# A small GpSimd write ahead of the first gather, and half of the second round of proposals later in VectorE's queue

## The chip, the cores and the metric

The kernel is one program on one core of a Trainium2 chip. The metric is the device time of the whole launch in microseconds (us). One core has five queues that concern us: TensorE (PE, with its weight loads PEld), VectorE (DVE), ScalarE (ACT), GpSimd (POOL) and SyncE (SP), and DMA queues which SP, ACT and POOL feed. [...]

## The reference, cut to what matters

```
scores = cap * tanh(q @ k.T / sqrt(64) / cap)      # 8 x 12 heads, 448 x 448
x = softmax(scores) @ v  -> (3584 tokens, 768)
logits = x @ w_gate                                 # 3584 x 8 experts
order = argsort(-logits.flatten())
for tok, e in order:                                # greedy: the largest logit first
    if assigned[tok] < 0 and counts[e] < 448: assigned[tok] = e; counts[e] += 1
for e in range(8):                                  # two products for the expert's 448 tokens
    out[mask_e] = relu(x[mask_e] @ w1[e]) @ w2[e]
```

## The kernel before

**Three stages.** Attention fills the first 350 us or so and writes x into a DRAM buffer `xs`. The routing finds, round by round, which expert is full first and which 448 tokens it gets. Each round starts with proposals: every token still free proposes itself to its best expert, as keys of three parts (`VA`, `VB`, `VC`, and the sums `K1`, `K2`); a search over the keys then finds the threshold. The FFN of the expert found in round p runs on TensorE while VectorE and ScalarE search round p+1 between the products.

**Proposals.** `propose_a` (12 VectorE instructions on all 3584 tokens, laid out 112 x 32) makes `m`, `P`, `kk`, `At`, `VA` and the raw parts `b` and `c`. `propose_b` (6 instructions, lines 514 to 518 and 526) makes `Bt`, `Ct`, `VB`, `VC`, `K1` and `K2` out of them. `propose` calls both, one behind the other. Which comes first needed: `VA` is turned by TensorE (line 536) and copied by VectorE (`VAt`, line 541) for the first search steps ("A"). `VB` and `VC` are turned by TensorE behind search step A0 (`flips`, into `psV`); `K1` and `K2` are used steps later.

**The seam between routing and FFN.** Round 0 ends with `idx` (line 722), the row numbers of expert 0's 448 tokens, from VectorE. GpSimd then issues the first gather: four indirect DMAs (line 872) of 128, 128, 128 and 64 rows of `xs` into the tiles `xg`. A dummy indirect DMA (`frow`, line 793) stands ahead of them. TensorE in the meantime runs 23 warming products (`warm(NW)`), turns `VA`, and then transposes the gathered rows, 128 at a time (`tx`, line 879). The first two of the four go through `cutx` (ScalarE makes the rounded part `xgh`, VectorE the rest `xgl`, lines 928 and 929), and `first` (line 895) multiplies them with expert 0's first weights; then come the other two, and `ffn1(0, 0)` (line 966), in which two more transposes (`xtr`, line 902) stand. The search steps of round 1 stand in TensorE's queue between the products of `ffn1`; each is one small product (line 572) that waits for VectorE's and ScalarE's comparisons (`cmpD`, lines 564 and 566, and `cmpA`, line 560), and its result is read by `fl` (line 576).

**What sets the order.** The order in each queue is the order of the Python calls: SP, PE, ACT, DVE and POOL are all under a manual schedule here. Waits come from data and from memory: a tile that takes the memory of an earlier one waits for that one's last readers and writers. `xg` takes memory that attention's tiles had, so the first gather waits not only for `idx` and the five DMA counters of the writes into `xs`, but also for a TensorE product of attention (line 236).

Of the kernel before, what the change touches and what calls it, by code (L numbers as in the profile page):

```python
# [6 lines left out]
F32=mybir.dt.float32; F32R=mybir.dt.float32r; BF16=mybir.dt.bfloat16; F16=mybir.dt.float16; I32=mybir.dt.int32; I16=mybir.dt.int16  # L7
# [378 lines left out]
class Routing:  # L386
# [357 lines left out]
    def phases0(s,wp,L,turned):  # L744
        HA=[7,10]; HB=3
        for p in range(s.E):
            s.hA=HA[min(p,len(HA))-1] if p else 7; s.hB=HB; s.na=2 if p<9 else 1
            s.cur=p
            if p:
                s.propose(L,0,s.NC)  # L750
                yield 30
            yield from (s.search(wp,turned if p==0 else ()) if p<s.E-1 else s.last(wp))
            yield -((p-1)*320+LK[p]) if p>1 else 4
            yield from s.finalise(wp,L,p<s.E-1)
# [3 lines left out]
def ffn_all(nc, tc, ctx, rt, xs, xz, wg, w1, w2, out, ident, E, wp, deferred, xctx, gen, avs):  # L758
# [16 lines left out]
    def need(p):  # L775
        while len(res)<=p: step()
# [51 lines left out]
    fp=ctx.enter_context(tc.tile_pool(name="fp",bufs=1))  # L828
# [33 lines left out]
    def newx(p):  # L862
        if p not in xgT: xgT[p]=(fp.tile([128,DC,C],F32R,name="xgh"),fp.tile([128,DC,C],F32R,name="xgl"))
    xgp=[fp.tile([128,2*DM],F32,name=f"xg{k}") for k in range(2)]
    row=lambda j,n=128: xgp[j//2][:n,j%2*DM:(j%2+1)*DM]
    nc.scalar.activation(xgp[1][64:128,DM:],rt.zero[64:128].broadcast_to([64,DM]),AF.Copy)
    def gather(p):
        if p>=E or p in xgs: return
        need(p)
        xgs[p]=1  # L870
        for j,(o,n) in enumerate(TS):
            g=nc.gpsimd.indirect_dma_start(out=row(j,n),out_offset=None,in_=xs,in_offset=bass.IndirectOffsetOnAxis(ap=res[p][0][:n,j:j+1],axis=0))
        return g
# [22 lines left out]
    def xtr(p,c):  # L896
        if p>=E or c is None: return
        newx(p)
        gather(p)
        ps=pt.tile([128,512],F32,name="psX")  # L900
        for j,(o,n) in enumerate(TS):
            nc.tensor.transpose(ps[:,o:o+128],row(j)[:,c*128:c*128+128],ident)
        cutx(p,c,ps)
# [21 lines left out]
    def cutx(p,c,ps,c0=0,c1=C):  # L925
        h,l=(t[:,c,c0:c1] for t in xgT[p])
        src=ps[:,c0:c1]
        nc.scalar.activation(h,src,AF.Copy)
        nc.vector.tensor_tensor(l,src,h.bitcast(F32),op=ALU.subtract)  # L929
# [5 lines left out]
    def tick(n=1):  # L935
        cnt[0]+=n; bc[0]+=n; now[0]+=n
        if bc[0]>=BG:
            if pend and not (cur[0]==FT-1 and 144<now[0]%320<316): bc[0]=0; scatter(*pend.pop(0))
        if len(res)>cur[0]+1 and cur[0]+1 not in xgs:
            bc[0]=0; n=cur[0]+1; gather(n)  # L940
            if n>=FT:
                xq.extend((now[0]+TD+TJ*j,lambda j=j: planes(j)) for j in range(4))
                xq.extend(((n-1)*320+248+8*f,lambda f=f: split1(n,f)) for f in range(2))
                o=(n-1)*320; g=now[0]-o; a=max(262,g+92); b=max(284,g+118)
                bg.extend((o+x,o+min(y,316),z) for x,y,z in ((a,a+18,lambda: cutt(n,0,0,3)),(a,a+34,lambda: cutt(n,0,3,6)),(b,b+(0 if n==FT else 26),lambda: cutt(n,1,0,3)),(b,b+(7 if n==FT else 22),lambda: cutt(n,1,3,6))))
        while xq and xq[0][0]<=now[0]: xq.pop(0)[1]()
        if bg and bg[0][1]<=now[0]: bg.pop(0)[2]()
        if cnt[0]>=hint[0]:
            cnt[0]=0; step()
    hh={}  # L950
    def ffn1(p,f,work):
        if f==0: hh[p]=f2.tile([128,FC,2*C],F32R,name="hh")
        wh,wl=spl.pop((p,1,f))
        xh,xl=xgT[p]
        ps=acc.pop(0) if p==0 and f==0 else ph.tile([128,512],F32,name="psH")
        m=0
        seq=[(c,k) for c in range(DC) for k in range(3)]
        if p==0 and f==0:
            seq=[(0,0),(0,2)]
            for c in range(1,DC): seq+=[(c,0),(c,2),(c-1,1)]  # L960
            seq+=[(DC-1,1)]
        elif p>=FT and f==0: seq=[(c,k) for c in range(DC) for k in (0,2)]+[(c,1) for c in range(DC)]
        for c,k in seq:
            a,b=((wh,xh),(wh,xl),(wl,xh))[k]
            o=256 if p==0 and f==0 and c<4 else 0
            nc.tensor.matmul(ps[:,o:C],a[:,c,:],b[:,c,o:],start=(m==0 and o==0),stop=(m==DC*3-1)); m+=1  # L966
            if p==0 and f==0 and k==1 and c<2: xtr(0,c+4)
            tick()
            for z in work.get(m,()): z()
        end[0]=now[0]  # L970
        h=hh[p][:,f,:]
        nc.scalar.activation(h[:,:C],ps[:,:C],AF.Relu)  # L972
        for a,b,d in ((384,448,448),(0,384,512)):
            nc.vector.scalar_tensor_tensor(h[:,d:d+b-a],ps[:,a:b],0.0,h[:,a:b].bitcast(F32),op0=ALU.max,op1=ALU.subtract)  # L974
# [35 lines left out]
    need(0)  # L1010
    WG=3; NW=23; WJ=4
    gather(0)
    tok=xgp[1][0:1,0:1]
    for i in range(WG,W1B): load1(0,i,tok)
# [8 lines left out]
    for p in range(E):  # L1023
        lastp=p==E-1; cur[0]=p
        for f in range(FC):
            if p==0:
                if f<2: load1(0,f+W1B)
                if f<7: load2(0,f+1)
                if 2<=f<4: load1(0,f+W1B)
            else:  # L1030
                if f<6: load2(p,f+2)
                if W1B<=f+W1B-1<FC: load1(p,f+W1B-1)
            work={}
            if f+2<FC and (p,1,f+2) not in spl: work[3]=[lambda: split1(p,f+2)]
            at={0:{1:[(11,0)],2:[(11,1)],3:[(11,2)],4:[(11,3)],5:[(11,4)],6:[(3,5),(11,6)],7:[(3,7)]},1:{k:[(11,k)] for k in range(FC)},2:{**{k:[(11,k)] for k in range(6)},6:[(8,6)]},E-1:{k:[(11,k)] for k in range(FC)}}.get(p,{k:[(11,k)] for k in range(5)})
            for m,n in at.get(f,()): work[m]=[lambda n=n: split2(p,n)]
            if p==1 and f==0: work[1]=[lambda: xtr(1,4)]; work[4]=[lambda: xtr(1,5)]
            ffn1(p,f,work)
# [30 lines left out]
def full(nc,tc,q,k,v,cap,wg,w1,w2,out):  # L1069
    with ExitStack() as ctx:  # L1070
# [27 lines left out]
        xr=xctx.enter_context(tc.tile_pool(name="xr",bufs=4,side="right"))  # L1098
        deferred=[lambda f=f: f((px,xr)) for f in deferred]
        ffn_all(nc,tc,ctx,r,xs,xz,wg,w1,w2,out,ident,8,wp,deferred,xctx,r.phases(wp,L1,turned),avs)  # L1100


# [25 lines left out]
```

## Time and profile before

| | |
|---|---|
| median of 3 runs | 880.43 us (880.41, 880.43, 881.24) |
| the profiled execution | 881.11 us |
| its span, first to last instruction | 879.3 us, mean granted TensorE clock 0.997 |
| busy in the span: PE, PEld, DVE, ACT, POOL | 857.2, 622.7, 586.6, 585.1, 374.6 us |

The span is what the trace covers; the 1.8 us between it and the execution's own time lie around it. TensorE is busy for 97% of the span, so nearly every us of the end time is TensorE's, but a busy share tells nothing of a single seam: what ends last there is read from the waits, the chain and the timeline of that place.

### The profile page before, as it was taken

What the parts mean: (1) busy time and instruction counts of PE and PEld (TensorE: products, weight loads), DVE (VectorE), ACT (ScalarE), POOL (GpSimd) and SP (SyncE); (2) the same over time, 40 slices, a digit from 0 to 9 for tenths busy, and PEclk for the clock granted to TensorE, in tenths of its full rate; (3) what the DMA queues carried; (4) which work ended last, traced back from release to release, by engine and by line L of the source; (5) the groups of instructions that cost most, each with busy time, mean ns of one, the idle gap of its engine ahead of it and who ended that gap; (6) DMA issues with size and microseconds to landing.
All of it is one profiled execution on the core that took longest, in us unless ns stands there. A gap on an engine that the chain in (4) does not pass through costs nothing.

```text
span 879.3 us, 17528 instructions
## 1 busy us (share of the span) xinstructions
PE 857.2 (97%) x6186; PEld 622.7 (71%) x6186; DVE 586.6 (67%) x2027; ACT 585.1 (67%) x832; POOL 374.6 (43%) x534
## 2 busy tenths in 40 slices
PE   7999999999999998899999999999999999999997
PEld 3334444444433335788989989989989989999997
DVE  3878988989897868876777777778767753130210
ACT  6999898889889878474483683664655745535521
POOL 8010000000000009583584495684774867756841
PEclk9999999999999999999999999999999999999999
DMA  9979997596986007770922874945936927928701
GB/s 133 160 122 145 185 142 157 96 184 93 233 167 104 1 19 255 223 234 22 310 83 73 228 240 131 261 148 173 308 88 177 298 73 198 305 73 241 226 10 54
DMA packets 339496, 140.05 MB, mean 159 GB/s; under 512 B 261232, under 2 KB 329456, under 8 KB 338896
## 3 DMA queue, kind: packets, MB, share of 16 engines
q1 hardware_dynamic: 328736, 109.03, 56.2%
q0 software_dynamic: 4688, 22.02, 7.4%
q10 hardware_dynamic: 5984, 7.88, 2.6%
q8 instruction: 48, 0.79, 0.4%
q14 instruction: 40, 0.33, 0.1%
HBM read 97.61 MB, written 33.03 MB: 149 GB/s over the span
## 4 chain that ended last, share of the span: by engine, by line
PE 85%; DVE 4%; issue 4%; ACT 4%; DMA 2%; POOL 1%; SPq 1%; POOLq 0%; DVEq 0%; ACTq 0%
PE psH L966 27%; PE psH L997 25%; PE psA L231 12%; PE psS L190 11%; PE psM L252 3%; ACT e L196 2%; PE psS L195 2%; PE psM L37 1%; ACT e L201 1%; DMA k<-in_k_dram 1%; DVE cmpD L564 1%; DMA xg<-xs,idx 1%; SPq L89 1%; PE psM L267 1%; PE psL L37 1%
## 5 line engine op out<-in xcount | busy, mean ns | idle before, releaser
L997 PE MATMUL psH<-w2h,hh 128*128 128x384 f32 x896 | 235.2, 340 | 0.0
L196 ACT ACTIVATE e<-psS 128x896 f32<-128x896 f32 x168 | 147.5, 910 | 30.4 <-PE psS L190 15.5
L997 PE MATMUL psH<-w2l,hh 128*128 128x384 f32 x512 | 166.0, 340 | 0.0
L997 PEld LDWEIGHTS psH<-w2h,hh 128*128 128x128 f32 x896 | 162.0, 189 | 0.1
L201 ACT ACTIVATE e<-e,bias 128x1792 f32<-128x1792 f32 (+2 forms) x74 | 147.3, 1992 | 1.8
L966 PE MATMUL psH<-xgh,w1h 128*128 128x448 f32 (+1 forms) x384 | 142.9, 372 | 0.1
L966 PE MATMUL psH<-xgh,w1l 128*128 128x448 f32 (+1 forms) x384 | 141.2, 368 | 0.0
L190 PE MATMUL psS<-tq,tk 64*64 64x448 f32 x1152 | 131.0, 549 | 5.9 <-ACT e L196 5.0
L966 PE MATMUL psH<-xgl,w1h 128*128 128x448 f32 (+1 forms) x384 | 136.7, 369 | 0.0
L850 POOL TENSOR_TENSOR w1l<-w1r,w1h 128x768 fp32r<-128x768 f32 x62 | 114.3, 1844 | 40.4 <-ACT w1h L843 34.6
L231 PE MATMUL psA<-e,nv 64*64 64x448 f32 x1104 | 121.1, 542 | 0.0
L850 POOL TENSOR_TENSOR w2l<-w2r,w2h 128x768 fp32r<-128x768 f32 x64 | 118.0, 1844 | 3.1 <-ACT w2h L843 3.1
L514 POOL TENSOR_SCALAR r_Bt<-r_b 112x4 f16<-112x4 int32 x1 | 0.2, 200 | 264.8 <-DVE rin L289 264.8
L207 DVE TENSOR_TENSOR es<-es,e 64x896 f32<-64x896 f32 (+2 forms) x70 | 96.0, 1372 | 2.7 <-ACT e L201 1.5
L997 PEld LDWEIGHTS psH<-w2l,hh 128*128 128x128 f32 x512 | 96.0, 189 | 0.1
L190 PEld LDWEIGHTS psS<-tq,tk 64*64 64x64 f32 x1152 | 43.1, 134 | 73.1 <-issue 36.8
L974 DVE SCALAR_TENSOR_TENSOR hh<-psH,hh 128x64 fp32r<-128x64 f32 (+1 forms) x128 | 44.1, 386 | 73.5 <-ACT hh L972 72.6
L972 ACT ACTIVATE hh<-psH 128x448 fp32r<-128x448 f32 x64 | 34.7, 543 | 84.3 <-PE psH L966 79.2
L231 PEld LDWEIGHTS psA<-e,nv 64*64 64x64 f32 x1104 | 44.8, 134 | 59.1 <-issue 52.0
L966 PEld LDWEIGHTS psH<-xgh,w1h 128*128 128x128 f32 x384 | 72.6, 189 | 5.6 <-ACT xgh L917 0.4
L966 PEld LDWEIGHTS psH<-xgh,w1l 128*128 128x128 f32 x384 | 72.4, 189 | 5.1
L966 PEld LDWEIGHTS psH<-xgl,w1h 128*128 128x128 f32 x384 | 72.4, 189 | 5.1 <-DVE xgl L929 0.2
(389 smaller groups left out, 1267.2 us busy)
## 6 DMA issues: line engine op xcount, KB each, us to landing
w1r<-in_moe_w_dram SPq DMA_DIRECT2D x64, 384.0 KB, 4.9
w2r<-in_moe_w_dram SPq DMA_DIRECT2D x64, 384.0 KB, 6.7
k<-in_k_dram SPq DMA_DIRECT2D x92, 112.0 KB, 3.5
q<-in_q_dram SPq DMA_DIRECT2D x92, 112.0 KB, 3.8
nv<-in_v_dram SPq DMA_DIRECT2D x72, 128.0 KB, 3.8
xz<-pl ACTq DMA_DIRECT2D x18, 384.0 KB, 2.9
xs<-xn SPq DMA_DIRECT2D x4, 1344.0 KB, 7.2
xd<-xT SPq DMA_DIRECT2D x2, 1344.0 KB, 6.1
```

The costliest lines, as they stand in the source:

```text
L37: nc.tensor.transpose(ps[:CP,j*128:(j+1)*128],xT[b][:,p,j*CP:(j+1)*CP],ident)
L190: for c in range(2): nc.tensor.matmul(ps[c*64:c*64+64,h,:S],tks[g,0][hp,o,u*128+c*64:u*128+c*64+64],tks[g,1][hp,o,:],start=True,stop=True)
L196: nc.scalar.activation(ev(g,r),ps[:,:,:S],AF.Tanh,scale=sr[0])
L201: act=lambda: nc.scalar.activation(e,e,AF.Exp,scale=sr[1],bias=bias)
L207: t=es_t[g]; add=lambda o,a,b: nc.vector.tensor_tensor(o,a,b,op=ALU.add)
L231: nc.tensor.matmul(avp[g,o][h*64:h*64+64,:S],lhs,rhs[hp,h,:],start=(j==0 and x==0),stop=j==3)
L252: nc.tensor.matmul(ps[g*32:g*32+32,:S],lhs,rhs,start=first,stop=last)
L850: (eng or nc.gpsimd).tensor_tensor(view(l),r,view(h).bitcast(F32),op=ALU.subtract)
L966: nc.tensor.matmul(ps[:,o:C],a[:,c,:],b[:,c,o:],start=(m==0 and o==0),stop=(m==DC*3-1)); m+=1
L972: nc.scalar.activation(h[:,:C],ps[:,:C],AF.Relu)
L974: nc.vector.scalar_tensor_tensor(h[:,d:d+b-a],ps[:,a:b],0.0,h[:,a:b].bitcast(F32),op0=ALU.max,op1=ALU.subtract)
L997: nc.tensor.matmul(ps[:,:HD],h[:,f,a:a+128],spl[p,2,hf,f//2][w][:,f%2,:],start=(m==0),stop=(m==nm-1))
```

## The change

Two edits. First, a tile `held` of one number is allocated in the pool of `xg`, right after it, and GpSimd writes a zero into it ahead of the first gather; nothing reads it. The tile also moves those that are allocated after it in the pools on that side (`xgh`, `xgl`, `pl`, `hh`, `on`) by 32 bytes. Second, `propose_b` of the second round (p = 1) is called later: no longer right behind `propose_a`, but inside `ffn1(0, 0)`, behind the second of the two transposes `xtr(0, 5)`. For p > 1 both halves stay together.

```diff
@@ phases0 @@
             if p:
-                s.propose(L,0,s.NC)
+                s.propose_a(L,0,s.NC)
+                if p>1: s.propose_b(0,s.NC)
                 yield 30
@@ ffn_all @@
     nc.scalar.activation(xgp[1][64:128,DM:],rt.zero[64:128].broadcast_to([64,DM]),AF.Copy)
+    held=fp.tile([1,1],F32,name="held"); nc.gpsimd.memset(held,0.0)
     def gather(p):
@@ ffn1 @@
-            if p==0 and f==0 and k==1 and c<2: xtr(0,c+4)
+            if p==0 and f==0 and k==1 and c<2:
+                xtr(0,c+4)
+                if c==1: rt.propose_b(0,rt.NC)
```

GpSimd's queue at the seam, before. In brackets stand the counters that a row waits for: DMAHW are DMA queues, DMASW the gathers' own, the others engines. The program puts all but the last of a bracket on bare wait instructions ahead of the row, one or two to each; the last name is the wait that the instruction itself holds.

```order
L52 TENSOR_TENSOR xn<-raw,rin 112x4x2x64 [waits DVE_49,Activation_49]
L793 DMA frow<-in_moe_w_gate_dram,zix 16x8 [waits DMAHW2_49,DMAHW7_49,DMAHW1_49,DMAHW0_49]
L872 DMA xg_4112<-xs,idx 128x768 [waits DMAHW2_49,DMAHW1_49,DMAHW3_49,DMAHW0_49,DMAHW7_49,DVE_49,PE_49]
L872 DMA xg_4112<-xs,idx 128x768
L872 DMA xg_4113<-xs,idx 128x768
L872 DMA xg_4113<-xs,idx 64x768
L788 COPY w1r<-xg_4113 1x1 [waits DMASW3_49]
```

The same place of the changed kernel (its lines are numbered one or two higher).

```order
L794 DMA frow<-in_moe_w_gate_dram,zix 16x8 [waits DMAHW2_49,DMAHW7_49,DMAHW1_49,DMAHW0_49]
L868 MEMSET held 1x1 [waits PE_49]
L874 DMA xg_4112<-xs,idx 128x768 [waits DMAHW2_49,DMAHW3_49,DMAHW1_49,DMAHW7_49,DMAHW0_49,DVE_49]
L874 DMA xg_4112<-xs,idx 128x768
L874 DMA xg_4113<-xs,idx 128x768
L874 DMA xg_4113<-xs,idx 64x768
L789 COPY w1r<-xg_4113 1x1 [waits DMASW3_49]
```

What moved: the wait for TensorE went from the gather to the new write. Before, the gather itself held the wait for TensorE, and the wait for `idx` (DVE) stood on the last of three bare wait instructions ahead of it. Now the gather itself holds the wait for `idx`, and the three bare ones ahead of it carry only DMA counters.

VectorE's queue behind `propose_a`, before:

```order
L509 TENSOR_SCALAR r_c<-r_u 112x32
L514 TENSOR_SCALAR r_Bt<-r_b 112x32
L515 TENSOR_SCALAR r_Ct<-r_c 112x32
L516 TENSOR_TENSOR r_VB<-r_P,r_Bt 112x256
L517 TENSOR_TENSOR r_VC<-r_P,r_Ct 112x256
L518 TENSOR_TENSOR r_K_339<-r_At,r_Bt 112x32
L526 SCALAR_TENSOR_TENSOR r_K_340<-r_kk,r_Ct 112x32
L541 CAST r_VAt<-psR 128x224
L850 TENSOR_TENSOR w1l<-w1r,w1h 128x768
L929 TENSOR_TENSOR xgl<-psX,xgh 128x256 x2
```

VectorE's queue in the changed kernel, from the last pieces of x to the first result of the search:

```order
L931 TENSOR_TENSOR xgl<-psX,xgh 128x448 x2
L514 TENSOR_SCALAR r_Bt<-r_b 112x32
L515 TENSOR_SCALAR r_Ct<-r_c 112x32
L516 TENSOR_TENSOR r_VB<-r_P,r_Bt 112x256
L517 TENSOR_TENSOR r_VC<-r_P,r_Ct 112x256
L518 TENSOR_TENSOR r_K_339<-r_At,r_Bt 112x32
L526 SCALAR_TENSOR_TENSOR r_K_340<-r_kk,r_Ct 112x32
L566 TENSOR_SCALAR cmpD,r_cd_324<-r_VAt,r_T0A 128x224 x2
L976 SCALAR_TENSOR_TENSOR hh<-psH,hh 128x64
L976 SCALAR_TENSOR_TENSOR hh<-psH,hh 128x384
L576 SCALAR_TENSOR_TENSOR fl,th<-psR,r_HA 128x4
```

What moved: the six instructions of `propose_b` left the place ahead of the copy of `VAt`, and stand now between the last two pieces `xgl` and the first comparisons `cmpD`. TensorE's, ScalarE's and SP's rows keep their order.

## Rows read from the trace of the kernel before

**Rows 1.** Waits of TensorE, 362 us to the end: total us, times, longest

```profile
PE psX L879 <- DMA xg<-xs,idx: 0.8, 1, 0.8
...
```

**Rows 2.** Chain that ended last, around the first gather: start us, us, what

```profile
362.12 0.19 DVE idx L722
...
363.43 0.99 POOL xg L872
364.42 0.30 issue
364.72 4.79 DMA xg<-xs,idx
...
369.56 0.44 PE psX L879 x2
```

**Rows 3.** Timeline of GpSimd and VectorE at the second and the eighth gather

```profile
419.34 0.19 DVE L722 TENSOR_REDUCE idx<-r_ixf 128x4 int32<-128x32 f32 x1
...
419.81 0.98 POOL L872 DMA_INDIRECT xg<-xs,idx  x1 [15.60 <-DVE zz L729]
...
785.82 0.19 DVE L722 TENSOR_REDUCE idx<-r_ixf 128x4 int32<-128x32 f32 x1
...
786.28 0.98 POOL L872 DMA_INDIRECT xg<-xs,idx  x1 [9.10 <-DVE idx L722]
```

**Rows 4.** Line 872 alone, 361.3 to 362 us: ns min/median/max, first and last start

```profile
L872 POOLq EVENT_SEMAPHORE  x2: 43/457/871, 361.4 to 361.5; - x2
```

**Rows 5.** Line 236 alone, the product of attention that the gather waits for

```profile
L236 PE MATMUL psX<-e,nvh x4: 536/562/587, 347.2 to 347.6; 64*64 64x448 f32 x4
```

**Rows 6.** Timeline of TensorE, 367 to 381 us

```profile
367.72 1.06 PE L807 MATMUL psR<-ident 128*128 128x128 f32 x8
...
372.04 0.38 PE L879 MATMUL psX<-ident,xg 128*128 128x128 f32 x2
...
377.99 0.18 PE L572 MATMUL psR<-r_cd,r_bo 128*128 128x4 bf16 x1
...
380.11 0.18 PE L572 MATMUL psR<-r_cd,r_bo 128*128 128x4 bf16 x1
```

**Rows 7.** Timeline of VectorE, 367 to 380 us

```profile
367.39 0.18 DVE L514 TENSOR_SCALAR r_Bt<-r_b 112x32 f16<-112x32 int32 x1
...
368.49 0.39 DVE L541 CAST r_VAt<-psR 128x224 f16<-128x224 f32 x1
368.79 0.95 DVE L850 TENSOR_TENSOR w1l<-w1r,w1h 128x768 fp32r<-128x768 f32 x1
370.35 0.76 DVE L929 TENSOR_TENSOR xgl<-psX,xgh 128x256 fp32r<-128x256 f32 x2 [0.60 <-ACT xgh L928]
...
375.02 1.38 DVE L929 TENSOR_TENSOR xgl<-psX,xgh 128x448 fp32r<-128x448 f32 x2 [0.72 <-ACT xgh L928]
376.32 0.44 DVE L566 TENSOR_SCALAR_CACHE_REDUCE cmpD<-r_VAt,r_T0A 128x224 bf16<-128x224 f16 x1
...
377.05 0.09 DVE L566 DVE_READ_ACCUMULATOR cmpD<-r_VAt,r_T0A 128x1 bf16 x1
377.55 0.69 DVE L974 SCALAR_TENSOR_TENSOR hh<-psH,hh 128x64 fp32r<-128x64 f32 x2 [0.41 <-ACT hh L972]
378.22 0.16 DVE L576 SCALAR_TENSOR_TENSOR fl<-psR,r_HA 128x4 f32<-128x4 f32 x1
...
379.30 0.09 DVE L566 DVE_READ_ACCUMULATOR cmpD<-r_VAt,r_HA 128x1 bf16 x1
```

**Rows 8.** Line 872 alone, the first gather's third DMA: issue, then landing

```profile
L872 POOL DMA_INDIRECT xg<-xs,idx x1: 1132/1132/1132, 366.2 to 366.2; - x1
...
DMA to landing us min/median/max: 5.6/5.6/5.6
```

**Rows 9.** DMA queues, 364 to 365 us: packets, MB, share of 16 engines

```profile
q1 hardware_dynamic: 304, 0.15, 61.0%
```

## The prediction, made before the changed kernel ran

> **What bounds the kernel now.** The waits of TensorE come first, because it is busy for 97% of the span. From 362 us to the end it loses its longest single wait, 0.8 us, to the first gather [rows 1]; the change touches this seam and nothing else, so the question is what these 0.8 us are made of. The chain that ended last tells it: `idx` starts at 362.12 and takes 0.19; GpSimd starts the first of four indirect DMAs only at 363.43; 0.99 and 0.30 later comes the second, at 364.72, and it lands after 4.79, at 369.51; TensorE transposes its rows from 369.56 [rows 2]. It could have begun earlier: its fill-in products from 367.72 take 1.06 and end at 368.78 [rows 6]. So 0.78 us stand open there (the 0.8 of the waits), and a gather that starts earlier by d closes min(d, 0.8) of them, a little more if the products' modelled ends are late.
>
> Between the start of `idx` and the start of the gather lie 1.31 us (363.43 - 362.12). At the second gather it is 0.47 (419.81 - 419.34), at the eighth 0.46 [rows 3]; the six between the first and the eighth all read 0.46 or 0.47. That is the anomaly: 0.85 us that only the first gather pays.
>
> **The first edit: where the wait stands.** Before, the wait for `idx` sits on the last of three bare wait instructions ahead of the gather. The trace shows it: of the two that start from 361.4 to 361.5 one takes 43 ns and the other 871 ns, that is, from 361.5 until about 362.37, just behind the end of `idx` at 362.31 [rows 4, 2]. From there to the gather's start are 1.06 us. In the seven later gathers the gather itself holds the wait for `idx`, and then it starts 0.28 behind the end of `idx` (0.47 - 0.19). I read the difference as time that an indirect DMA needs between coming to the head of GpSimd's queue and starting: where it holds the wait itself, this passes while it waits. The change gives the first gather the form of the seven others. TensorE's product, for which `held` waits instead, had run by 348.3 [rows 5], long before; so the write costs GpSimd one short instruction in a stretch in which it only waits for `idx`, and no new wait arises. Queued behind it are only the gather's own waits.
>
> One thing keeps me from the full sum: the gather must have stood at the head long enough. The bare waits for the writes into `xs` end near 361.5 [rows 4], the end of `idx` is 362.31, so it stands there 0.8 us. Of the 1.06 that it needed, 0.28 come behind the wait anyway; the other 0.78 just fit. I take d = 0.82, with 0.85 as the upper bound and 0 as the lower (if the 0.85 is the price of the first gather and not of the wait's place).
>
> [...]
>
> Does the landing follow the issue? The three other DMAs follow at fixed steps on GpSimd, so all four start 0.82 earlier. The load of expert 0's first weights is the neighbour: between 364 and 365 it still takes 61% of the DMA engines [rows 9], and the first rows would now flow from about 364.4 and meet its tail. I leave 0.1 for that: the second DMA lands some 0.75 to 0.85 earlier, at 368.66 to 368.76, and TensorE, free at 368.78, starts its transposes at about 368.75 in place of 369.56. **Term one: -0.8.**
>
> What is late next? The third DMA starts at 366.2 and lands 5.6 later, at 371.8 [rows 8]; its rows are transposed at 372.04 [rows 6]. It has 0.2 us in hand, and moves along by itself. Were the landing to move by only 0.5 us, TensorE would win 0.7 here.
>
> **The second edit: six instructions later.** On VectorE `propose_b` takes from 367.39 to the copy of `VAt` at 368.49, so 1.10 us for six instructions [rows 7].
>
> Ahead of the FFN their absence helps only if VectorE is late there. Now `w1l` ends at 369.74 and the first `xgl` starts at 370.35, 0.60 later [rows 7]. With x 0.8 earlier, that `xgl` would be due at 369.55, and with the six still ahead of it would wait 0.2 us for `w1l`. Moving them takes this away: the copy is then bound by TensorE's turning of `VA`, and `w1l` ends near 368.7. I put its gain on TensorE's path at 0 to 0.2 and book none of it apart from term one, which needs it.
>
> In the new place they cost. VectorE ends its last two `xgl` at 376.40 and the first two comparisons run from 376.32 to 377.14 (the second one's read-out, 377.05 and 0.09) [rows 7]. The product of the search step that needs them stands in TensorE's queue at 377.99 [rows 6]. That is 0.85 us in hand, 0.80 when 0.05 for the signal is taken off. Now 1.10 us of other work go in ahead of the comparisons, and both the last `xgl` and TensorE's place shift alike with x; so TensorE has to wait 1.10 - 0.80 = 0.30 us for the comparisons, with all the products of `ffn1` queued behind. **Term two: +0.3**, whatever the first edit does.
>
> Does it go on? `hh` runs behind the comparisons, 0.69 us, and `fl` behind it. By the old clock less 0.8: comparisons end at 377.44, `hh` at 378.13, then `fl`, and from the start of `fl` to the end of the next comparisons are 1.17 (379.39 - 378.22) [rows 7], so 379.30. The next search product comes 2.12 us after the first (380.11 - 377.99) [rows 6], and that one is now at 377.49, so at 379.61: 0.3 in hand, no second stall. `VB` and `VC`, which TensorE turns behind the first search product, are written before the comparisons even start. `K1` and `K2` are wanted steps later. From there the order is the old one, and TensorE has no wait behind it on which a DMA ends, so the difference goes through to the end.
>
> The 32 bytes by which `xgh`, `hh` and `on` move cost nothing that a row shows; I price them at 0 and keep them as a rival.
>
> **Sum.** -0.8 + 0.3 = -0.5 us. Against the profiled execution that is 881.11 - 0.5 = 880.6. Its own time lies 0.7 above the median of the runs shown, two of which are 880.4 and one 881.2; so for the median I forecast 880.43 - 0.5 = 879.9. That is 0.06%, and a measurement of this kernel can tell about 0.2% (1.8 us) from no change: no measurable change.
>
> **The rivals.**
>
> *The gather doesn't start earlier* (the change doesn't do what it says). For it: the first gather is the only slow one and also the only first one. Against: a dummy indirect DMA ran ahead of it, and the 871 ns wait ends just where the lead starts. Then term one is 0 and term two stays: 881.4 in the profile, 880.7 in the median, **slower** by 0.3. It decides from the point at which the gather wins less than 0.3. Chance 0.1. [...]
>
> *The gather starts earlier but its rows don't*: the weights' tail holds the DMA engines. By the 61% of one us at most 0.6 could be lost, which leaves -0.2 for term one and +0.1 in sum: 880.5 in the median. Chance 0.1.
>
> *The comparisons are not late*: if VectorE gains more ahead of them than I count, term two is 0 and the median is 879.6. Against: `xgl` is tied to x and not to VectorE. Chance 0.08.
>
> *Something that is not at the seam*: the moved tiles cost or win something in each of the seven other experts. To be measurable it would have to be 0.25 us in each; no row speaks for it. Chance 0.04 for each side.
>
> The forecast itself (0.3 to 0.8 faster) has 0.64.
>
> **How the numbers follow.** All cases at the seam lie between 880.43 - 0.85 and 880.43 + 0.3, so 879.6 to 880.7. The runs of one kernel spread by 0.8 us here, and a median of three can fall on either end: that takes it to 879.0 on the one side and 881.4 on the other. Faster by over 0.2% and slower by over 0.2% are left to the moved tiles alone, 0.04 each; the rest, 0.92, is no measurable change.
>
> **What would show it.** The first gather starts 0.46 or 0.47 behind the start of `idx`, and its last bare wait is short (right if so; at 1.3 the first edit failed). TensorE's wait for the gather, 0.8 now, is under 0.1. In its place stands a new wait of the first search product for `cmpD`, about 0.3. The six instructions stand behind the last `xgl` in 1.1 us. The span is 0.5 shorter, and all of it is there by 380 us: the distance from the second search product to the end is the same in both. If that distance differs by over 0.5, the seam is not where the difference comes from, and my reasoning is wrong.

## The result, and the profile after

The changed kernel takes 885.6 us in the median of six runs (884.91 to 887.27). The kernel before, run beside it on the same chip, takes 880.41. The ratio is 1.0061 with a 95% interval of 1.0051 to 1.0072: the kernel is slower by 5.2 us, about six tenths of a per cent. The forecast was 879.9 us in a range of 879.0 to 881.4, so it missed in size and in sign.

The profiled execution took 885.37 us with a span of 883.6 us, 4.3 longer than before. The mean granted clock is 1.000 of full speed, where it was 0.997, so a slower clock is not the reason.

At the seam, the queues did what the edits ask. GpSimd, then VectorE, timeline of the changed kernel (start us, us, engine, line, operation, tiles; in brackets the idle time ahead and what ended it):

```profile
357.63 0.09 POOL L868 MEMSET held<- 1x1 f32 x1
362.40 0.98 POOL L874 DMA_INDIRECT xg<-xs,idx  x1 [4.68 <-DVE zz L729]
363.69 1.19 POOL L874 DMA_INDIRECT xg<-xs,idx  x1 [0.30 <-issue]
```

```profile
361.93 0.19 DVE L722 TENSOR_REDUCE idx<-r_ixf 128x4 int32<-128x32 f32 x1
...
376.37 0.18 DVE L514 TENSOR_SCALAR r_Bt<-r_b 112x32 f16<-112x32 int32 x1
...
377.37 0.19 DVE L526 SCALAR_TENSOR_TENSOR r_K<-r_kk,r_Ct 112x32 f32<-112x32 f16 x1
377.47 0.44 DVE L566 TENSOR_SCALAR_CACHE_REDUCE cmpD<-r_VAt,r_T0A 128x224 bf16<-128x224 f16 x1
```

The first gather now starts 0.47 us behind the start of `idx` (362.40 - 361.93), where [rows 2] had 1.31. (Its bracket names `zz`, the instruction behind `idx`; the eighth gather in [rows 3] names `idx` and has the same lead.) The bare wait that [rows 4] showed with 871 ns is gone: the two recorded from 360.9 to 361.3 take 43 ns each. The six instructions of `propose_b` fill 376.37 to 377.47, 1.10 us.

But TensorE gets nothing of the earlier start. Its longest waits from 362 us to the end, to be held against [rows 1]:

```profile
PE psX L881 <- DMA xg<-xs,idx: 0.7, 2, 0.5
PE psR L572 <- ACT hh L976: 0.4, 1, 0.4
PE psR L572 <- DVE cmpD L566: 0.2, 1, 0.2
```

The chain that ended last, around the first gather, to be held against [rows 2]:

```profile
361.93 0.19 DVE idx L722
...
362.40 0.98 POOL xg L874
363.38 0.30 issue
363.69 5.88 DMA xg<-xs,idx
...
369.61 0.44 PE psX L881 x2
...
377.46 0.84 ACT w1h L844
378.30 0.04 issue
378.35 0.18 PE psR L572
```

The second DMA was issued earlier and took longer, 5.88 us in place of 4.79, so its rows were transposed 7.68 us behind the start of `idx`, where it had been 7.44. The wait for the gather, which was to fall under 0.1, is still 0.7 us, now in two parts. The first search product came at 378.35, which is 8.74 behind these transposes, where it had been 8.43 [rows 2, 6].

That is a few tenths of a microsecond. The other 4 us lie behind the seam, where no instruction was touched. From the second search product to the end of the span the changed kernel takes 503.1 us (883.6 - 380.48) and the kernel before 499.2 (879.3 - 380.11, [rows 6]). No wait stands there. TensorE is simply slower product by product: on the page its time in the first layer has grown in all three groups. First the changed kernel, then the kernel before (this part of its page was not shown above); busy us and mean ns of one:

```profile
L968 PE MATMUL psH<-xgh,w1h 128*128 128x448 f32 (+1 forms) x384 | 143.7, 374 | 0.1
L968 PE MATMUL psH<-xgh,w1l 128*128 128x448 f32 (+1 forms) x384 | 142.0, 370 | 0.0
```

```profile
L966 PE MATMUL psH<-xgh,w1h 128*128 128x448 f32 (+1 forms) x384 | 142.9, 372 | 0.1
L966 PE MATMUL psH<-xgh,w1l 128*128 128x448 f32 (+1 forms) x384 | 141.2, 368 | 0.0
```

The means hardly show it, because products overlap: the first row has a mean of 374 ns a product, while in the last expert each starts 206.6 ns behind the one before (below). The chain that ended last shows the pace in the last expert, where TensorE runs one product behind the other: the second layer of the sixth and seventh expert's stretch (174 products in a piece) and the whole first layer of the eighth (144 products). First before, then after:

```profile
724.32 30.29 PE psH L997 x174
784.77 30.29 PE psH L997 x174
815.06 29.19 PE psH L966 x144
```

```profile
726.36 30.83 PE psH L1001 x174
787.87 30.83 PE psH L1001 x174
818.70 29.75 PE psH L968 x144
```

29.19 us for 144 products is 202.7 ns from one to the next; 29.75 is 206.6. 30.29 for 174 is 174.1 ns, and 30.83 is 177.2. The same products, by the same instructions, take 2% longer, and the granted clock is no lower. The eighth expert's second layer alone keeps its pace (30.35 us before, 30.33 after). Added up from the start times of TensorE's products, the changed kernel is 0.04 us late at the start of `ffn1(0, 0)`, loses 0.54 in the first layer of expert 0, 2.47 in the first layers of the seven others and 1.14 in the second layers: 4.19 us at the start of the last product.

### The profile page after: what moved, and what is told of

It reads as the page before. It is cut to its first block, busy times and chain, and to the rows that moved or that the text cites. A ratio compares the mean times of both kernels' runs of the same rounds, so it can differ in the third digit from the quotient of the medians.

```text
span 883.6 us, 17528 instructions
## 1 busy us (share of the span) xinstructions
PE 859.9 (97%) x6186; PEld 623.3 (71%) x6186; DVE 585.7 (66%) x2027; ACT 585.4 (66%) x832; POOL 374.1 (42%) x535
## 4 chain that ended last, share of the span: by engine, by line
PE 83%; issue 4%; DVE 4%; DMA 3%; ACT 3%; SPq 2%; POOL 1%; POOLq 0%; ACTq 0%; DVEq 0%
PE psH L968 27%; PE psH L1001 25%; PE psA L231 11%; PE psS L190 10%; PE psM L252 3%; SPq L89 2%; PE psS L195 2%; DMA k<-in_k_dram 2%; ACT e L196 1%; PE psM L37 1%; DMA q<-in_q_dram 1%; DVE es L207 1%; ACT e L201 1%; DMA xg<-xs,idx 1%; DVE cmpD L564 1%
```

## The experiments

**Theory A** is that the tile `held` slows the products by moving `xgh`, `xgl` and `hh` by 32 bytes. The rival, called Theory B in the expectations, is that the edits at the seam do it, by another order or another state of things that lasts to the end. Theory C is that TensorE's pace differs from run to run. The second time in each result is that of the kernel before, run beside it on the same chip. A diff is against the kernel before, and the two edits of the change are not shown again.

**The tile alone, `pad_only`.** It is allocated and never written; no instruction is added or moved.

```diff
+    held=fp.tile([1,1],F32,name="held")
```

> The kernel before, with a tile of one number allocated where the change has its tile, but nothing written into it and no other edit: xgh, xgl, pl, hh, on and y3 lie 32 bytes further, and no instruction differs. Theory A (the address): the products of the first FFN layer take 206 to 207 ns each instead of 202 to 203, and the time is 884 to 886 us, as after the change. Theory B (something at the seam between routing and FFN puts the rest out of step): no difference, 880.4 us. Theory C (TensorE's pace differs from run to run): somewhere between, and not the same in the rounds.

885.1 us against 880.96, ratio 1.0043 (1.0029 to 1.0057). The tile alone brings 4.1 us, and its profile has the span of the changed kernel within 0.2 us (883.4 and 883.6) and the last expert's first layer at 29.75.

**Both edits without the tile, `no_pad`.** GpSimd's write goes into `gap`, a tile that exists already, so nothing moves.

```diff
+    nc.gpsimd.memset(gap,0.0)
```

> Both edits of the change, but the small write goes into the tile gap, which exists already, so no tile moves. Gap waits also for the writes into xs, so the gather's own wait for idx comes a little later behind it. Theory A: the products of the first layer take 202 to 203 ns as before the change, and only the seam differs: 880.4 to 880.9 us. Theory B: 884 to 886 us.

881.72 us against 880.96, ratio 1.0005 (0.9996 to 1.0015), and 29.19 us in the last first layer. So the edits cost nothing that can be told, and the rival falls. Theory C falls as well, as far as the profiles reach: the last expert's first layer reads 29.19 us in the kernel before, `no_pad`, `move_only`, `all32` and `h64`, and 29.75 or 29.76 in the changed kernel, `pad_only` and `x32`.

**Both edits with a tile of 64 bytes, `pad64`.**

```diff
+    held=fp.tile([1,16],F32,name="held"); nc.gpsimd.memset(held[:,0:1],0.0)
```

> The change with a tile of 16 numbers instead of one, so that the tiles behind it lie 64 bytes further than before, not 32. Theory A, if what counts is the place within 64 bytes: 880.4 to 880.9 us and 202 to 203 ns; theory A, if the distance between two tiles counts in another way: any time, with a pace of its own. Theory B: 884 to 886 us.

878.89 us against 880.96, ratio 0.9974 (0.9964 to 0.9983). A larger step doesn't cost more, it wins: 32 bytes lose 5 us and 64 bytes gain 2.

**The second edit alone, `move_only`** (`propose_b` later, no write by GpSimd).

> Only the second edit: the second half of the second round's proposals later, no small write and no moved tile. By the sum in the prediction VectorE is 0.3 us late for the first product of the search, so 880.7 us, with a wait of 0.3 for cmpD that the kernel before doesn't have. Theory A: 202 to 203 ns per product of the first layer. Theory B: 884 us or more if this edit is what puts the rest out of step.

881.0 us against 880.96, ratio 0.9997 (0.9988 to 1.0007). Nothing measurable in the time; what it does in the trace stands below, with the prediction's second term.

**x and hh apart, `x32` and `h32`.** In `x32` x moves by 32 bytes and `hh` by 128, in `h32` only `hh` (and `on`) by 32.

```diff
# x32
+    f2.tile([1,24],F32,name="pad2")
...
+    fp.tile([1,8],F32,name="pad")
# h32
+    f2.tile([1,8],F32,name="pad2")
```

> The kernel before with two unwritten tiles and no other edit: xgh, xgl and pl lie 32 bytes further, as after the change, while hh, on and y3 lie 128 bytes further. If the rows of x are what counts (read 448 columns at a time by the first layer): 206 to 207 ns per product of that layer and 884 to 885.5 us. If hh is what counts: 202 to 203 ns and 880.4 to 881 us.

> The kernel before with one unwritten tile behind gap: hh, on and y3 lie 32 bytes further, as after the change, and xgh and xgl lie where they did. If the rows of x are what counts: 202 to 203 ns per product of the first layer, and at most the second layer's small part (the profile of the change has it 0.3 to 0.5 us longer in four of the eight experts): 880.4 to 882 us. If hh is what counts: 884 us or more.

`x32` took 886.16 us against 880.3, ratio 1.0068 (1.0051 to 1.0085); `h32` 883.16, ratio 1.0032 (1.0021 to 1.0044). Both layers have a share. One thing didn't fit: in `h32` x has not moved, and yet the first layers of experts 6 and 7 ran at the slow pace.

**The 64 bytes alone, and everything moved together: `pad64_only` and `all32`.** In `all32` a pad of 32 bytes ahead of all the FFN's tiles moves the weights along with x, `hh` and `on`.

```diff
# pad64_only
+    fp.tile([1,16],F32,name="pad")
# all32
+    wb=ctx.enter_context(tc.tile_pool(name="wb",bufs=1)); wb.tile([1,8],F32,name="pad")
```

> The kernel before with an unwritten tile of 64 bytes where the change has its tile, and neither of the change's edits. If the gain of the 64 bytes comes from the address alone: 878.0 to 879.3 us, as with both edits, and 200 to 201 ns per product of the first layer. If it needs the edits at the seam: 880.4 us or more.

> The kernel before with an unwritten tile of 32 bytes ahead of the weights: weights, x, hh and on all lie 32 bytes further, so xgh stands where it stands after the change, and at the old distance from the weights w1h and w1l. If the distance of x from the weights counts (two reads that meet): 202 to 203 ns per product of the first layer and 880.4 to 881 us. If the place of x itself counts: 206 to 207 ns and 884 to 885.5 us.

`pad64_only` took 877.83 us against 880.3, ratio 0.9972 (0.9962 to 0.9982): with no edit at all it is faster than both kernels, by 2.5 us. `all32` took 880.77, ratio 1.0005 (0.9995 to 1.0014), with the sums of its products where they were (the first table below). So it is not the address of x that counts, but its distance from the weights.

**More distances: `pad96_only`, `pad128_only`, `x64` and `h64`.** The first two are `pad64_only` with 24 and 32 numbers; `x64` moves x by 64 and `hh` by 128 bytes, `h64` moves `hh` alone by 64.

```diff
# x64
+    f2.tile([1,16],F32,name="pad2")
...
+    fp.tile([1,16],F32,name="pad")
# h64
+    f2.tile([1,16],F32,name="pad2")
```

> The kernel before with an unwritten tile of 96 bytes where the change has its tile, and no other edit. 32 bytes cost 4 to 5 us and 64 gave 2.5. If x and its weights run freely at every distance that isn't a bad one: 877 to 878 us and 200 ns per product of the first layer. If 32 and 96 are alike (an odd number of 32 bytes): 884 to 886 us and 206 to 207 ns.

> The same with 128 bytes. If the place counts only within 128 bytes: as the kernel before, 880.3 us and 202 to 203 ns per product of the first layer. If the distance counts over a longer stretch: another pace, 200 or 207 ns, and 877.5 or 885 us.

> Two unwritten tiles: xgh, xgl and pl lie 64 bytes further, and hh, on and y3 128 bytes further. If the gain of the 64 bytes is one of x and its weights alone: 200 ns per product of the first layer and 877.5 to 878.5 us, the second layer as with 128 bytes alone. If hh must move by 64 as well: 880 us or more.

> One unwritten tile behind gap: hh, on and y3 lie 64 bytes further, xgh and xgl where they did. If the first layer's pace is set by x and its weights alone: 202 to 203 ns and 880 us. If the pace of the second layer is handed on to the first (as the six last stretches of the kernel with hh 32 bytes further seem to show): 200 ns in some of the stretches, and 878 to 880 us.

Against 881.19 us: `pad96_only` 885.79, 1.0054 (1.0036 to 1.0072); `pad128_only` 885.18, 1.0052 (1.0034 to 1.007); `x64` 881.87, 1.0011 (1.0 to 1.0021); `h64` 880.5, 0.9992 (0.9982 to 1.0002). The last expert's first layer in the chain of each, in this order, with `pad64_only` and `h32` behind them:

```profile
818.22 29.57 PE psH L967 x144
```

```profile
818.37 29.38 PE psH L967 x144
```

```profile
815.95 28.81 PE psH L968 x144
```

```profile
813.36 29.19 PE psH L967 x144
```

```profile
812.16 28.82 PE psH L967 x144
```

```profile
816.88 29.75 PE psH L967 x144
```

Divided by 144 these are 205.3, 204.0, 200.1, 202.7, 200.1 and 206.6 ns.

**All the kernels in one table.** The program's addresses give each kernel two distances: that of `xgh` and `xgl` from the weights `w1h`, `w1l` (all their buffers stand at multiples of 256 bytes from one another), and that of `hh` from `w2h`, `w2l`, both modulo 256. The sums are worked out from the start times of TensorE's products: first layers of experts 1 to 7 (counted from 0), and second layers of all eight. The settled pace is the time from one start to the next in the long runs of products with nothing between them.

| x from w1, B | kernels | first layers, us | settled pace, ns |
|---|---|---|---|
| 0 | before, `no_pad`, `move_only`, `all32`, `h64` | 213.7 to 214.3 | 202.7; some shorter runs 206.5 |
| 0 | `h32` | 215.2 | 202.7; two experts 206.6 |
| 32 | after, `pad_only`, `x32` | 216.0 to 216.8 | 206.6; expert 1 partly at 200 |
| 64 | `pad64`, `pad64_only`, `x64` | 211.4 to 212.0 | 200.1 |
| 96 | `pad96_only` | 215.9 | 205.3 |
| 128 | `pad128_only` | 214.6 | 204.0 |

| hh from w2, B | kernels | second layers, us |
|---|---|---|
| 32 | before, `no_pad`, `move_only`, `all32` | 255.8 to 256.1 |
| 64 | after, `pad_only`, `h32` | 257.2 to 257.7 |
| 96 | `pad64`, `pad64_only`, `h64` | 255.3 to 255.4 |
| 128 | `pad96_only` | 258.3 |
| 160 | `x32`, `x64`, `pad128_only` | 259.2 |

Each layer's sum follows its own distance, whatever the other layer and the seam do; only the first layers of `h32` lie 0.9 us above the others of their distance. `x64` explains itself by it: its first layers gain 2.8 us and its second layers lose 3.1.

**The products by themselves: `sweep` and `sweep_busy`.** Is it TensorE alone, or does the distance only decide with which other engine's traffic it collides? Behind their loads both kernels hold nothing but products of the two shapes, 72 for each distance, and in the second one VectorE and ScalarE work beside them. Each was executed once.

```diff
+LAYER1=[(32*k,0) for k in range(16)]+[(32*k,32*k) for k in (1,2,3)]+[(0,32*k) for k in (1,2,3)]+[(32*k,0) for k in (0,1,2,3,4)]
...
+                        w=wo//4+(2*f+kw)*768+c*128; x=xo//4+kx*2688+c*448
+                        nc.tensor.matmul(ps[:,:448],W[:,w:w+128],X[:,x:x+448],start=m==0,stop=m==17); m+=1
```

> This kernel leaves out attention, routing and the FFN, and has nothing but TensorE products of the FFN's two shapes, 72 in a row for each place of the operands: 128x128 weights and 448 columns of x (first layer), 128x128 of hh and 384 columns (second layer), with no other engine at work. x stands 0 to 480 bytes behind its first place in steps of 32; then weights and x move together by 32, 64, 96; then the weights alone; then x by 0 to 128 again. Theory A (the pace is a matter of TensorE and the two operands' addresses alone): the steps of the kernel come back here: 202.6 ns at 0, about 206 at 32, 200.3 at 64, 205 at 96, 204 at 128, the same at the repeat, and the joint moves all at 202.6. Rival (the address only sets with whom TensorE's reads meet, that is, writes and reads of the other engines): one pace at every place, within 0.5 ns, some 199 to 203.

> The same products, also without attention, routing and FFN, while VectorE subtracts and ScalarE copies 128x1024 numbers without a pause in tiles that TensorE doesn't read. Theory A: the same pace at each place as in the quiet run, within 0.5 ns. Rival: differences by place of 2 to 6 ns stand here and not in the quiet run, or the pace is everywhere 2 ns or more above it.

The chain of `sweep`, the first nine distances (0 to 256 bytes; each piece also holds a slower beginning of some 0.1 us, so that pieces are compared with one another):

```profile
30.95 14.99 PE ps L45 x72
...
45.94 14.50 PE ps L45 x72
...
60.45 14.52 PE ps L45 x72
...
74.98 14.89 PE ps L45 x72
...
89.87 14.79 PE ps L45 x72
...
104.67 14.97 PE ps L45 x72
...
119.65 14.66 PE ps L45 x72
...
134.32 14.82 PE ps L45 x72
...
149.15 14.97 PE ps L45 x72
```

From start to start the settled paces are 206.7, 200.0, 200.0, 205.4, 203.9, 206.7, 202.2 and 204.4 ns at 0 to 224 bytes, and from 256 bytes on the row repeats within 0.1 ns. Weights and x moved together by 32, 64 and 96 read 202.7 each time; the weights alone moved by 32 and 64 read 204.4 and 202.2, as x does at 224 and 192, but moved by 96 they read 200.0, where x at 160 reads 206.7. For the second layer's shape four distances, 0 to 96, read 173.3 ns and 128 reads 176.1, which is what `pad96_only` pays (176.0).

In `sweep_busy` VectorE and ScalarE are at work for 428.0 and 427.2 of 440 us while TensorE runs:

```profile
60.00:500.00 440.00, 440.00 (x2239) 411.96 (x2238) 427.99 (x350) 427.21 (x404) 0.00 (x0) 1.00 0.00 1
```

and the settled pace of each distance is that of the quiet run within 0.2 ns. So the rival falls: the pace goes with the places of TensorE's two operands, with VectorE and ScalarE at work or not. GpSimd and DMA traffic beside the products were not tried apart from the kernel itself. Of Theory A's numbers, 64, 96 and 128 bytes came as expected; 0 read 206.7 at its first turn and 202.7 at its second, and 32 read 200 where the changed kernel runs at 206.6.

**Two paces at one distance: `sweep_start`.** Executed once as well: eight stretches at each of four distances, with one product of another length ahead of each, so that they start at different moments.

```diff
+MARKS=(8,16,24,32,48,64,96,128)
+LAYER1=[(32*k,n) for k in (0,1,2,4) for n in MARKS]
```

> As sweep, first-layer products alone (attention, routing and the FFN are left out), at four places of x (0, 32, 64 and 128 bytes), each eight times: ahead of every stretch of 72 stands one product of 8, 16, 24, 32, 48, 64, 96 or 128 columns, so that the same products at the same place start at eight different moments against the one before. Theory A with two paces at a place (which of the two a stretch falls into is settled at its start and then holds): place 0 shows both 202.7 and 206.7, place 32 both 200 and 206.7, place 64 only 200. Rival (the place alone decides, and the two readings of place 0 in sweep, 206.7 and 202.7, came from something that a start does not change): one pace at each place whatever stands ahead of it, 202.7, 200, 200 and 204.1.

The chain of `sweep_start`: four stretches at distance 0, then one each at 32, 64 and 128.

```profile
30.97 14.99 PE ps L45 x72
...
45.97 14.69 PE ps L45 x72
...
60.66 14.98 PE ps L45 x72
...
75.66 14.68 PE ps L45 x72
...
164.42 14.97 PE ps L45 x72
...
283.80 14.51 PE ps L45 x72
...
385.44 14.79 PE ps L45 x72
```

Distance 0 reads 206.7 in three stretches of eight and 202.7 in five, each kept to the stretch's end. Distance 64 reads 200.0 in all eight, 128 reads 203.9 to 204.1. Distance 32 reads 206.7 eight times, where `sweep` had 200.0 each time. So at distances 0 and 32 (and by the two readings of `sweep` at 160) two paces were read; at distance 0 they differ from start to start within one run, and each held through the 72 products of its stretch. The simple rival (one pace at a distance) falls. The expectation that both would turn up at 32 within this run failed; they do over the two runs together. `h32` fits now: its x stands at distance 0, which has a slower pace too, and two experts ran at it. That moving `hh` shifted the moments at which these layers start is the likely reason, but was not tested. The kernel before holds both paces as well. A run of 40 products in the sixth expert's first layer, before and then in `h64`, whose x stands at the same distance:

```profile
710.55 8.35 PE psH L966 x40
```

```profile
709.03 8.22 PE psH L967 x40
```

From start to start these products take 206.5 and 202.9 ns. The second layer shows the same thing with `hh` at 64: in the changed kernel, `pad_only` and `h32` the sixth and seventh expert run at 176.7 ns and the eighth at 173.3, which is what `sweep` reads there. So part of the cost of the 32 bytes hangs on how the layers happen to start.

## Why the prediction was wrong, point by point

**The step that failed** is the sentence "The 32 bytes by which `xgh`, `hh` and `on` move cost nothing that a row shows; I price them at 0". No row showed a price because every row of one trace has the same distance; the one sign in the trace before was the run of 40 products above, 206.5 ns where 202.7 is the rule, with no wait in it. With both edits and no moved tile the time stays (`no_pad`, 1.0005); with the moved tile and no edit it rises by 4.1 us (`pad_only`). The prediction even had the threshold for each of the seven other experts, "it would have to be 0.25 us in each"; it is 0.35 in a first layer (2.47 / 7) and 0.14 in a second one (1.14 / 8). To rate that at 0.04 on each side was a guess, not a reading: the trace could bound a stall, but not the pace of products at an address that it had never seen.

**The first edit: start right, gain wrong.** The gather starts 0.47 behind `idx` whenever it holds the wait itself (after, `no_pad`, `pad64`: 0.46 or 0.47), and 1.31 behind it where the edit is missing (`move_only`, `pad_only`). That the difference is time which an indirect DMA needs at the head of GpSimd's queue was the author's reading; no run shows it by itself. But "the second DMA lands some 0.75 to 0.85 earlier" did not come. Over the profiles, the second pair of transposes starts 7.35 to 8.40 us behind `idx` in the eleven without the edit (median 7.68) and 7.53 to 7.68 in the three with it. In the changed kernel it was the landing. By the landing times in the trace, 15 of the second DMA's 16 parts were in by 368.44, 0.77 earlier than before (369.21; 0.19 of it is that `idx` came earlier). The last came at 369.56, where it had been 369.52, and TensorE started 0.05 behind it. A possible reason stands in the DMA queues, 366 to 367 us, in a queue that the profile calls instruction; first after, then before (packets, MB, share of 16 engines):

```profile
q8 instruction: 1, 0.02, 8.6%
```

```profile
q8 instruction: 1, 0.02, 6.1%
```

Its one packet, of 16 KB, takes 1.35 to 1.44 us in the three profiles with the first edit and 0.97 to 1.01 in the eleven others. In the changed kernel it ends at 367.46, and the first DMA's last part lands at 367.47. That the two hold each other up was not tested. In `no_pad` and `pad64` TensorE stood still earlier, between its first and second transpose:

```profile
366.86 0.29 PE L881 MATMUL psX<-ident,xg 128*128 128x128 f32 x1
367.88 0.33 PE L881 MATMUL psX<-ident,xg 128*128 128x128 f32 x1 [0.74 <-PE psR L536]
```

The same wait stands in `pad_only` and `move_only` (0.88 and 0.75), so it belongs to neither edit. The trace puts it down to a product of TensorE itself, which by its own row in `no_pad` had ended at 367.02; what it really is stays open, for the traces of `no_pad` and `pad64` hold only 6 and 7 landings of the first DMA's 16 parts. Term one measured about 0, not -0.8. The rival that had the gather start earlier and its rows not (the weights' tail, chance 0.1) is the nearest to it, but the tail is an unlikely reason: in the changed kernel the last packet of the weights' queue ends at 365.95, 3.6 us ahead of the last landing.

**The second edit: right.** From the second pair of transposes to the first search product the ten profiles with `propose_b` in its old place take 8.36 to 8.45 us (mean 8.40), the four with it later 8.66 to 8.74 (mean 8.71): +0.31, where +0.3 was forecast. The chain names `w1h` on ScalarE in front of that product and not `cmpD`. Both end together there, at 378.29. The read-out of `cmpD` after, and `w1h` before:

```profile
378.20 0.09 DVE L566 DVE_READ_ACCUMULATOR cmpD<-r_VAt,r_T0A 128x1 bf16 x1
```

```profile
377.41 0.84 ACT L843 ACTIVATE w1h<-w1r 128x768 fp32r<-128x768 f32 x1
```

Before, `w1h` ended at 378.25, and the product started at 377.99 all the same [rows 6]. So it does not wait for `w1h`, and it is `cmpD` that was late, as forecast. The waits have no row for it: by the modelled ends of the products ahead TensorE is idle for 0.13 us only, though the product starts 0.3 late. The 0.05 taken off for the signal is what the chain before shows between VectorE's `ev` and TensorE's product (361.63 to 361.68). There is no second stall, as forecast: the second search product follows the first after 2.11 to 2.13 us in these four, and after 2.12 before.

**The sum corrected.** In the two profiles the stretch ahead of `idx` gives -0.19, the way to the second transposes +0.24 in place of -0.8, the way to the first search product +0.31, and the pace of the products +3.84 (0.23 of the 0.54 in expert 0's first layer, 2.47 and 1.14): +4.20, against 4.19 read at the last product and 4.3 at the end of the span. The medians differ by 5.2; the 0.9 that is left is about the spread of the runs. The seam's own terms add up to +0.36, so without the moved tile, too, the change would not have been faster. The prediction named the observation that would refute it (the stretch from the second search product to the end, equal within 0.5); it differs by 3.9.

**A better version.** `pad64_only`, the kernel before with one unwritten tile of 64 bytes, runs at 877.83 us (0.9972). The two edits on top of it (`pad64`, 0.9974) add nothing that can be told.

## What to carry to other kernels

Here a new tile of one number moved the tiles allocated behind it by 32 bytes, and in this kernel, whose time is TensorE's products, that alone cost up to 0.7 per cent or won 0.3: compare an edit with a version that makes the same allocation and nothing else, or put the write into a tile that exists. When the time changes where no instruction was touched and no wait appears, divide a long run of equal products by their number in both traces before looking for a stall. A gain that depends on when a DMA's last part lands is to be checked at the landing and at the engine that waits for it, not at the start of the transfer.

## What the runs showed of the hardware

In these runs the pace of TensorE's products depends on the distance between its two operands in SBUF: 200.0 to 206.7 ns for 448 columns in `sweep`, where the row repeats within 0.1 ns from 256 bytes on, and 173.3 to 176.1 for 384. In `sweep_busy`, with VectorE and ScalarE at work for 428.0 and 427.2 of 440 us, no pace moved by more than 0.2 ns. For 448 columns two paces were read at distances 0, 32 and 160; at 0, `sweep_start` has 206.7 in three stretches and 202.7 in five, each kept to the stretch's end. For 384 columns the changed kernel has two at 64, 173.3 and 176.7.

If the operands' places didn't matter to each other, there would be one pace for 448 columns; `sweep` shows a spread of 3.3%. Why the distance matters, and what in the start picks one of two paces, no run here shows.
